# A decode step on one core: w2 loaded in four pieces in place of five, and two more unused products between the wo groups

## The chip, the core and the metric

The kernel runs on one core of one Trainium2 chip. The metric is the device time of one execution in microseconds (us). Before the change it was 84.56 us, the median of four runs (84.45, 84.47, 84.64, 84.67). A separate execution was profiled; everything that is read from the profile belongs to that one.

## The reference, cut to what matters

Four rows (a batch of 4, one token each, width 512) go through a conditioned transformer block: attention over the last 1,024 positions of a key and value cache with 32 query heads and 8 key heads, then a dense layer of width 1,792 with a ReLU. Scales, shifts and gates come from a conditioning vector `c`.

```python
mod = (_silu(c) @ w_mod).reshape(c.shape[0], 6, 1, -1)
sa, ca, ga, sb, cb, gb = (mod[:, i] for i in range(6))
h = _layernorm(x) * (1 + ca) + sa
x = x + ga * _A_ref(h, k_cache, v_cache, wq, wo)     # attention, then @ wo
h = _layernorm(x) * (1 + cb) + sb
h = jnp.einsum('bsd,df->bsf', h, w1)                 # 512 -> 1792
h = jnp.maximum(h, 0)
x = x + gb * jnp.einsum('bsf,fd->bsd', h, w2)        # 1792 -> 512
```

All weights and caches are bf16. Together the kernel reads 32 MB once.

## The kernel before

All large loads are issued by SyncE, in one queue and in the order in which they are written down: `w_mod`, two pieces of k, `wq`, six more pieces of k, eight of v, four of `wo` (one for each group g, line 121), `w1` (line 126), and `w2` in the five transfers of `W2_CHUNKS` (lines 128 to 133). A transfer is spread over the core's DMA engines. `w1` and `w2` lie in one tile, `w12`, which the profile calls `w`.

The contraction over 1,792 is cut into FT = 14 blocks of 128, numbered m = 0 to 13. A transfer of e blocks that begins at block m0 lays e consecutive rows of `w2` on each partition, so block m of that transfer holds every e-th row. The columns of `w1` that feed block m must be picked in the same way; `w1_cols` (line 477) does this with a stride of e. Thus `W2_CHUNKS` sets three things: the size of the transfers, which blocks arrive together, and the stride at which the weights of the first dense product are read.

The order of work on TensorE, VectorE, ScalarE and GpSimd is the order of the program text (a manual schedule); waits between engines are put in by the framework. What matters here is the last part, from the products with `wo` on:

1. Groups g = 0 and 1 of `wo` are multiplied with the attention result as the weights (line 427), four products side by side. The result is copied (lines 431, 432) and folded by fp32 products (line 436). Groups 2 and 3 are multiplied the other way round, with `wo` as the weights: 32 products a group of 32 columns each (line 440).
2. `keep_busy` (lines 444 to 448 and 462) issues products whose result nobody reads: an identity times columns of `wo`, into `sc_ps`, which held the attention scores earlier. It is called twice with the widths 512 and 256.
3. VectorE forms the residual and the second layer norm from `y_ps` (lines 451 to 475); TensorE sums over partitions (line 457) and puts the residual into the output's layout (`x12_ps`, line 461).
4. `ffn1` (line 489) multiplies with `w1`, once for blocks 0 to 7 and once for 8 to 13, 4 products a block (line 495); VectorE applies the norm's scale, adds, and takes the maximum with 0 (lines 498, 500, 501), which gives `uT32`.
5. The product with `w2` runs block by block through `closing` (line 192). One block is four products of 128 columns: two for x = 0 and two for x = 1, the two of a pair side by side on different quarters of the array. If `closing` is given two blocks of different halves, four products run side by side. The blocks of `ZUP` = (0, 1, 2, 3, 6, 7, 8) are summed in the upper half of the array, into `za_ps`; the others in the lower half, into `z_ps` (line 482).
6. After block 8, the last of `ZUP`, ScalarE copies `za_ps` to `zc` (line 513) and VectorE multiplies it with the gate and adds the residual (lines 514, 515). After block 13 VectorE multiplies `z_ps` with the gate (`zg`, line 520) and adds both (`res`, line 522). Two small DMAs write the result (lines 524, 525).

The order of the blocks in step 5 is written out by hand:

```python
    for ms in [(0,), (1,), (2, 4), (3, 5), (6,), (7,), (8, 9)]:
        closing([zpart(m) for m in ms])
    zc = work.tile([2 * CG, DH2], f32, name="zc")
    nc.scalar.copy(out=zc[:], in_=za_ps[2 * CG:P, :])
    ...
    for m in range(10, FT):
        closing([zpart(m)])
```

Of the kernel before, what the change touches and what calls it, by code (L numbers as in the profile page):

```python
# [17 lines left out]
def kernel(  # L18
# [14 lines left out]
    nc = tc.nc  # L33
# [8 lines left out]
    FT = Dff // P  # L42
# [63 lines left out]
    for h in range(Hkv):  # L106
        vt_ = kvpool.tile([P, NI, Dh], bf16, tag="kv", name=f"v{h}")
        nc.sync.dma_start(
            out=vt_[:].rearrange("p j d -> p (j d)"),
# [6 lines left out]
    NP = Hkv // 2  # L116
    wo_sb = wts.tile([P, NP, NL, D], bf16, tag="big", name="wo_sb")
# [7 lines left out]
    w2_sb = w12[:, DT * Dff:DT * Dff + FT * D].rearrange("p (m n) -> p m n", m=FT)  # L125
    nc.sync.dma_start(out=w1_sb, in_=B_w1.rearrange("(p t) n -> p t n", t=DT))

    W2_CHUNKS = [(0, 4), (4, 4), (8, 3), (11, 2), (13, 1)]
    assert sum(e for _, e in W2_CHUNKS) == FT
    w2_dst = w12[:, DT * Dff:DT * Dff + FT * D]  # L130
    for (m0, e) in W2_CHUNKS:
        nc.sync.dma_start(out=w2_dst[:, m0 * D:(m0 + e) * D],
# [4 lines left out]
    ident_bf = const.tile([P, P], bf16, name="ident_bf")  # L137
# [54 lines left out]
    def closing(parts):  # L192
        for x in range(NX):
            for (ps, q, j, src, rhs, start, stop, cols) in parts:
                for g in range(2):
                    q0 = (q + g) * CG
                    nc.tensor.matmul(out=ps[q0:q0 + CG, cols], lhsT=rows(src, j, x), rhs=rhs(2 * x + g),  # L197
                                     start=start and x == 0, stop=stop and x == NX - 1, tile_position=(0, q0))
# [21 lines left out]
    sc_ps = psS.tile([P, W], f32, tag="s", name="sc_ps")  # L220
# [39 lines left out]
    for t in range(DT):  # L260
        for k in range(4):
            nc.tensor.matmul(out=m4_ps[k * CG:(k + 1) * CG, :], lhsT=rows(siluT32, t, 0), rhs=wmod_sb[:, t, k * D:(k + 1) * D],
                             start=(t == 0), stop=(t == DT - 1), tile_position=(0, k * CG))
    for t in range(DT):
        nc.tensor.matmul(out=m5_ps[:], lhsT=rows(siluT32, t, 0), rhs=wmod_sb[:, t, 4 * D:5 * D],
                         start=(t == 0), stop=(t == DT - 1), tile_position=(0, 0))
# [8 lines left out]
    for t in range(DT):  # L275
        nc.tensor.matmul(out=mT[:, t, 0:4, :].rearrange("p k b -> p (k b)"), lhsT=m4_sb[:, t, :], rhs=ident_m[:],
                         start=True, stop=True)
# [45 lines left out]
    for t in range(DT):  # L323
        for hq in range(Hq):
            nc.tensor.matmul(out=qT_v[:, hq, :], lhsT=wq_sb[:, t, hq * Dh:(hq + 1) * Dh], rhs=hT[:, t, :],  # L325
                             start=(t == 0 and hq == 0), stop=(t == DT - 1 and hq == Hq - 1))
    for par in range(2):
        dst = qpad_s[:, :, par * NHW * CG:(par + 1) * NHW * CG].rearrange("p b (h c) -> p b h c", h=NHW)
        nc.vector.tensor_copy(  # L329
            out=dst[:, :, :, 16 * par:16 * par + rep],  # L330
# [78 lines left out]
    for l in range(NL):  # L409
        for a in range(2):  # L410
            for rh in range(rep // 2):
                q0 = (2 * a + rh) * CG
                nc.tensor.matmul(out=o4_ps[q0:q0 + CG, l], lhsT=sel_o[:, l].rearrange("p s d -> p (s d)"),
                                 rhs=oT_sb[:, a::2, :, :, 2 * rh:2 * rh + 2], start=True, stop=True,
# [4 lines left out]
                                   op0=ALU.mult, op1=ALU.add)  # L419


    GM = NP // 2
    y4_ps = psA.tile([P, D], f32, tag="t", name="y4_ps")
    for g in range(GM):
        for l in range(NL):
            q0 = l % 4 * CG
            nc.tensor.matmul(out=y4_ps[q0:q0 + CG, :], lhsT=o4[:, l, g % 2, g // 2, :], rhs=wo_sb[:, g, l, :],  # L427
                             start=(g == 0 and l < 4), stop=(g == GM - 1 and l >= 4), tile_position=(0, q0))
    y4 = work.tile([P, DT, P], f32, name="y4")
# [5 lines left out]
    for t in range(DT):  # L435
        nc.tensor.matmul(out=y32_ps[:, t, :], lhsT=y4[:, t, :], rhs=sel_b[:], start=(t == 0), stop=False)  # L436
    for g in range(GM, NP):
        for l in range(NL):
            for m in range(DT):
                nc.tensor.matmul(out=y32_ps[:, m, :], lhsT=wo_sb[:, g, l, m::DT], rhs=o4[:, l, g % 2, g // 2, :],  # L440
                                 start=False, stop=(g == NP - 1 and l == NL - 1 and m == DT - 1))


    def keep_busy(widths):
        for w in widths:
            nc.tensor.matmul(out=sc_ps[:, 0:w], lhsT=ident_bf[:], rhs=wo_sb[:, NP - 1, 0, 0:w], start=True, stop=True)

    keep_busy((512, 256))

    yT = work.tile([P, DT, B], f32, name="yT")  # L450
# [7 lines left out]
                     start=True, stop=True)  # L458
    x12_ps = psA.tile([2 * CG, DH2], f32, tag="t", name="x12_ps")
    for t in range(DT):  # L460
        closing([(x12_ps, 0, t, xs2, lambda j: ident_f[:, j * (P // NH):(j + 1) * (P // NH)], True, True, slice(t, None, DT))])
    keep_busy((512, 256))
    me = work.tile([P, 2, B], f32, name="me")
    nc.vector.tensor_reduce(out=me[:], in_=s2_ps[:].rearrange("p s t b -> p s b t"), axis=AX.X, op=ALU.add)
# [12 lines left out]
    def w1_cols(t, m):  # L477
        m0, e = [ch for ch in W2_CHUNKS if ch[0] <= m][-1]
        return w1_sb[:, t, m0 * P + m - m0:(m0 + e) * P:e]
# [9 lines left out]
    def ffn1(m0, m1):  # L489

        u4_ps = psA.tile([P, m1 - m0, NR, 2, B], f32, tag="t", name=f"u_ps_{m0}")
        u_ps = u4_ps[:, :, 0]
        for m in range(m0, m1):
            for t in range(DT):
                nc.tensor.matmul(out=u4_ps[:, m - m0].rearrange("p n s b -> p n (s b)"), lhsT=w1_cols(t, m),
                                 rhs=ab[:, t].rearrange("p s b -> p (s b)").unsqueeze(1).to_broadcast([P, NR, 2 * B]), start=(t == 0), stop=(t == DT - 1))
        us = work.tile([P, m1 - m0, B], f32, name=f"us_{m0}")
        nc.vector.tensor_tensor(out=us[:], in0=u_ps[:, :, 0, :], in1=rstd2[:].unsqueeze(1).to_broadcast([P, m1 - m0, B]),
                                op=ALU.mult)
        nc.vector.tensor_tensor(out=us[:], in0=us[:], in1=u_ps[:, :, 1, :], op=ALU.add)  # L500
        nc.vector.tensor_scalar_max(out=put(uT32[:, m0:m1, :]), in0=us[:], scalar1=0.0)

    def zpart(m):
        mine = ZUP if m in ZUP else ZLOW
        return (za_ps if m in ZUP else z_ps, 2 if m in ZUP else 0, m, uT32, lambda j: w2_sb[:, m, j * DH2:(j + 1) * DH2],
                m == mine[0], m == mine[-1], slice(None))

    for (m0, m1) in [(0, 8), (8, FT)]:
        ffn1(m0, m1)
    for ms in [(0,), (1,), (2, 4), (3, 5), (6,), (7,), (8, 9)]:  # L510
        closing([zpart(m) for m in ms])
    zc = work.tile([2 * CG, DH2], f32, name="zc")
    nc.scalar.copy(out=zc[:], in_=za_ps[2 * CG:P, :])
    nc.vector.tensor_tensor(out=zc[:], in0=zc[:], in1=gb2[:], op=ALU.mult)
    nc.vector.tensor_tensor(out=zc[:], in0=zc[:], in1=x12_ps[:], op=ALU.add)
    for m in range(10, FT):
        closing([zpart(m)])

    zg = work.tile([2 * CG, DH2], f32, name="zg")
# [36 lines left out]
```

## Time and profile before

| | |
|---|---|
| median of four runs | 84.56 us (84.45 to 84.67) |
| the profiled execution's own time | 84.53 us |
| its span, first to last instruction | 82.7 us |
| TensorE busy | 57.0 us, 69% |
| VectorE busy | 26.5 us, 32% |
| ScalarE busy | 23.9 us, 29% |
| mean granted TensorE clock | 0.81 of full speed |
| mean DMA rate | 388 GB/s over the span |

Some 1.8 us of the execution's own time lie outside the span. "Busy" is the time in which an engine's instructions are recorded as running; matmuls overlap, so a busy TensorE is not one at its peak. "Idle before, releaser" names what an engine waited for. PE is TensorE's products, PEld its weight loads, DVE VectorE, ACT ScalarE, SPq the queue of DMA issues on SyncE. Times in a timeline are us from the start of the span.

### The profile page before, as it was taken

How to read it: one execution, taken by the hardware profiler on the slowest of the kernel's cores; microseconds unless marked ns; L12 is line 12 of the kernel's file. 1: busy time of each engine (PE TensorE's matmuls, PEld its weight loads, DVE VectorE, ACT ScalarE, POOL GpSimd, SP SyncE). 2: the span in 40 equal slices, each digit the busy share in tenths (PEclk: the TensorE clock that was granted, in tenths of full speed). 3: DMA queues.
4: the chain of work that ended last, by engine and by line, in shares of the span. 5: the costliest groups of instructions: out<-in, count | busy, mean ns of one | idle time of the engine just before them, and what ended most of it. 6: DMA issues, size and time to landing. Idle time of an engine off the chain costs nothing.

```text
span 82.7 us, 2381 instructions
## 1 busy us (share of the span) xinstructions
PE 57.0 (69%) x1068; PEld 47.0 (57%) x1068; DVE 26.5 (32%) x76; ACT 23.9 (29%) x38; POOL 5.9 (7%) x21
## 2 busy tenths in 40 slices
PE   0001006999982798999999960999928579999740
PEld 0000006996772792997778810899918229877520
DVE  0211300348223201066654566952000320051450
ACT  3201001664302000477887745840100010002010
POOL 5895000000000000000000000000000000000000
PEclk9999999999996555599999999759855555555999
DMA  3799899998979999999999999999999999989700
GB/s 41 285 486 428 376 424 436 570 412 349 507 325 412 436 420 432 412 436 424 432 408 436 424 428 412 436 428 424 424 420 428 428 408 458 445 364 408 293 24 2
DMA packets 4257, 32.14 MB, mean 388 GB/s; under 512 B 528, under 2 KB 664, under 8 KB 1304
## 3 DMA queue, kind: packets, MB, share of 16 engines
q1 hardware_dynamic: 4192, 31.99, 92.6%
q8 instruction: 8, 0.13, 0.6%
q0 software_dynamic: 32, 0.00, 0.0%
q10 hardware_dynamic: 24, 0.01, 0.0%
q14 instruction: 1, 0.01, 0.0%
HBM read 31.99 MB, written 0.00 MB: 387 GB/s over the span
## 4 chain that ended last, share of the span: by engine, by line
DMA 93%; SPq 2%; PE 1%; DVE 1%; issue 0%
DMA v<-in_A_v_cache_dram 34%; DMA wo_sb<-in_A_wo_dram 24%; DMA w<-in_B_w_dram 19%; DMA k<-in_A_k_cache_dram 16%; PE z_ps L197 1%; SPq L86 1%; SPq L96 0%; SPq L95 0%; DVE zg L520 0%; DVE res L522 0%
## 5 line engine op out<-in xcount | busy, mean ns | idle before, releaser
L228 PE MATMUL ktp<-ident_k,k 128*128 128x128 bf16 x256 | 19.0, 246 | 5.6 <-DMA k<-in_A_k_cache_dram 5.6
L228 PEld LDWEIGHTS <-k 128*128 128x128 bf16 x256 | 17.9, 113 | 8.2 <-DMA k<-in_A_k_cache_dram 5.7
L233 ACT COPY kT<-ktp 128x1024 bf16<-128x1024 bf16 x16 | 15.6, 1015 | 18.0 <-PE ktp L228 16.9
L231 DVE COPY kT<-ktp 128x1024 bf16<-128x1024 bf16 x16 | 11.1, 691 | 17.0 <-PE ktp L228 16.7
L363 PE MATMUL oT_ps<-pT,v 128*128 128x16 bf16 x256 | 7.1, 172 | 1.6 <-issue 1.6
L363 PEld LDWEIGHTS <-v 128*128 128x128 bf16 x256 | 7.1, 100 | 1.7 <-issue 1.7
L240 PE MATMUL sc_ps<-kT,qpad 128*32 128x512 bf16 x64 | 5.6, 445 | 0.4 <-DVE qpad L329 0.4
L203 PE MATMUL tp<-ident_bf,cx_sb 8*128 8x8 bf16 x4 | 0.3, 174 | 7.2 <-DMA cx_sb<-in_A_x_dram 7.2
L380 PE MATMUL pT_ps<-ident_bf,p_rep 128*128 128x128 bf16 x32 | 3.3, 286 | 2.9 <-DVE p_rep L374 2.9
L380 PEld LDWEIGHTS <-p_rep 128*128 128x128 bf16 x32 | 2.9, 133 | 3.3 <-DVE p_rep L374 3.3
L325 PE MATMUL qT_ps<-hT,wq_sb 128*128 128x4 bf16 x128 | 3.6, 166 | 1.4 <-DVE ab L318 1.4
L325 PEld LDWEIGHTS <-wq_sb 128*128 128x128 bf16 x128 | 3.5, 104 | 1.5 <-DMA wq_sb<-in_A_wq_dram 1.5
L203 PEld LDWEIGHTS <-cx_sb 8*128 8x128 bf16 x4 | 0.2, 114 | 7.2 <-DMA cx_sb<-in_A_x_dram 7.2
L432 ACT COPY y<-y_ps 128x256 f32<-128x256 f32 x1 | 0.4, 372 | 9.0 <-DVE y L431 9.0
L374 DVE TENSOR_TENSOR p_rep<-e_sb,mi 128x512 int32<-128x512 int32 x4 | 2.5, 686 | 0.7 <-ACT e_sb L369 0.7
L405 DVE TENSOR_TENSOR oT_sb<-oT_ps,rb 128x128 bf16<-128x128 f32 x1 | 0.3, 292 | 7.5 <-PE oT_ps L363 7.5
L436 PEld LDWEIGHTS y_ps<-sel_b,y 128*128 128x128 f32 x8 | 1.8, 329 | 1.4 <-DVE y L431 1.4
L427 PE MATMUL y_ps<-wo_sb,o 128*32 128x512 bf16 x16 | 1.9, 626 | 0.9 <-DVE o L418 0.9
L440 PEld LDWEIGHTS <-wo_sb 128*128 128x128 bf16 x64 | 2.5, 121 | 0.0
L240 PEld LDWEIGHTS <-qpad 128*32 128x32 bf16 x64 | 1.3, 103 | 2.2 <-DVE qpad L329 0.7
L369 ACT ACTIVATE e_sb<-sc_ps,nb 128x256 bf16<-128x256 f32 x4 | 1.8, 471 | 2.1 <-DVE nb L346 2.1
L440 PE MATMUL y_ps<-o,wo_sb 128*128 128x32 bf16 x64 | 2.4, 195 | 0.0
(115 smaller groups left out, 56.7 us busy)
## 6 DMA issues: line engine op xcount, KB each, us to landing
k<-in_A_k_cache_dram SPq DMA_DIRECT2D x8, 1024.0 KB, 28.1
v<-in_A_v_cache_dram SPq DMA_DIRECT2D x8, 1024.0 KB, 19.6
wq_sb<-in_A_wq_dram SPq DMA_DIRECT2D x1, 4096.0 KB, 23.6
wo_sb<-in_A_wo_dram SPq DMA_DIRECT2D x4, 1024.0 KB, 19.9
wmod_sb<-in_w_mod_dram SPq DMA_DIRECT2D x1, 2304.0 KB, 9.4
w<-in_B_w_dram SPq DMA_DIRECT2D x1, 1792.0 KB
w<-in_B_w_dram SPq DMA_DIRECT2D x2, 512.0 KB, 19.8
wmod_sb<-in_w_mod_dram SPq DMA_DIRECT2D x1, 768.0 KB, 4.4
```

Of the source, the lines that this page charges most:

```text
L228: nc.tensor.transpose(out=tp[:, ii, :], in_=k_tiles[gi][:, iq * IQ + ii, :], identity=ident_k)
L231: nc.vector.tensor_copy(out=dst, in_=tp[:])
L233: nc.scalar.copy(out=dst, in_=tp[:])
L240: nc.tensor.matmul(out=sc_ps[hw * CG:(hw + 1) * CG, half * HALF:(half + 1) * HALF], lhsT=qpad[:, b, par, hw, :], rhs=kT[:, half * (NI // 2 ...
L325: nc.tensor.matmul(out=qT_v[:, hq, :], lhsT=wq_sb[:, t, hq * Dh:(hq + 1) * Dh], rhs=hT[:, t, :], start=(t == 0 and hq == 0), stop=(t == DT ...
L363: nc.tensor.matmul(out=oT_ps[:, hw, par].rearrange("p b r -> p (b r)"), lhsT=v_tiles[h][:, i, :], rhs=pT[:, i, c0:c0 + B * rep], start=(fi ...
L369: nc.scalar.activation(out=e_sb[:, ws].rearrange("q (u k e) -> q u k e", k=KC, e=2), in_=sc_ps[:, ws].rearrange("q (u e k) -> q u k e", e= ...
L374: nc.vector.tensor_tensor(out=p_w[:, ws, :], in0=e_w[:, ws].unsqueeze(2).to_broadcast([P, WQ // 2, B]), in1=mi4[:].unsqueeze(1).to_broadca ...
L380: nc.tensor.transpose(out=tp[:, ii, :], in_=p_rep[:, i // 2, :, i % 2], identity=ident_bf[:])
L427: nc.tensor.matmul(out=y4_ps[q0:q0 + CG, :], lhsT=o4[:, l, g % 2, g // 2, :], rhs=wo_sb[:, g, l, :], start=(g == 0 and l < 4), stop=(g == ...
L436: nc.tensor.matmul(out=y32_ps[:, t, :], lhsT=y4[:, t, :], rhs=sel_b[:], start=(t == 0), stop=False)
L440: nc.tensor.matmul(out=y32_ps[:, m, :], lhsT=wo_sb[:, g, l, m::DT], rhs=o4[:, l, g % 2, g // 2, :], start=False, stop=(g == NP - 1 and l = ...
```

## The change

`w2` is loaded in transfers of 6, 5, 2 and 1 blocks in place of 4, 4, 3, 2 and 1. The stride of the `w1` columns follows. Blocks 9 and 10 move: block 9 is paired with 7 and block 10 with 8, so that the copy of `za_ps` stands after blocks 0 to 10 in the text. `keep_busy` is defined earlier, takes a group number, and is called once more: two products of 256 and 128 columns, reading group 0 of `wo`, between the groups 2 and 3 of line 440.

```diff
-    W2_CHUNKS = [(0, 4), (4, 4), (8, 3), (11, 2), (13, 1)]
+    W2_CHUNKS = [(0, 6), (6, 5), (11, 2), (13, 1)]
...
+    def keep_busy(widths, g=NP - 1):
+        for w in widths:
+            nc.tensor.matmul(out=sc_ps[:, 0:w], lhsT=ident_bf[:], rhs=wo_sb[:, g, 0, 0:w], start=True, stop=True)
...
     for g in range(GM, NP):
+        if g > GM:
+            keep_busy((256, 128), 0)
         for l in range(NL):
             for m in range(DT):
                 nc.tensor.matmul(out=y32_ps[:, m, :], lhsT=wo_sb[:, g, l, m::DT], rhs=o4[:, l, g % 2, g // 2, :],
                                  start=False, stop=(g == NP - 1 and l == NL - 1 and m == DT - 1))
-
-
-    def keep_busy(widths):
-        for w in widths:
-            nc.tensor.matmul(out=sc_ps[:, 0:w], lhsT=ident_bf[:], rhs=wo_sb[:, NP - 1, 0, 0:w], start=True, stop=True)
...
-    for ms in [(0,), (1,), (2, 4), (3, 5), (6,), (7,), (8, 9)]:
+    for ms in [(0,), (1,), (2, 4), (3, 5), (6,), (7, 9), (8, 10)]:
         closing([zpart(m) for m in ms])
...
-    for m in range(10, FT):
+    for m in range(11, FT):
         closing([zpart(m)])
```

## The prediction, made before the changed kernel ran

> **What bounds the kernel now.** I read the chain of waits first, then the page's slices, then the timeline of the last 6 us, since every edit but one acts there.
>
> ```profile
> by line: DMA v<-in_A_v_cache_dram 33.9%; DMA wo_sb<-in_A_wo_dram 24.1%; DMA w<-in_B_w_dram 18.8%; DMA k<-in_A_k_cache_dram 15.9%; PE z_ps L197 0.8%; SPq L86 0.7%; SPq L96 0.5%; SPq L95 0.5%; issue 0.4%; DVE zg L520 0.4%; DVE res L522 0.3%
> ...
> 63.55 15.55 DMA w<-in_B_w_dram
> 79.10 0.04 issue
> 79.14 0.65 PE z_ps L197 x12
> ```
>
> 93% of the span is one queue of loads; only the last 1.3 us before the output belong to engines. What counts is when the last pieces of w2 land, and what follows.
>
> ```profile
> 77.76 0.39 PE L197 MATMUL za_ps<-w,uT 128*32 128x128 bf16 x8
> 78.50 0.23 PE L197 MATMUL za_ps<-w,uT 128*32 128x128 bf16 x2 [0.35 <-DMA w<-in_B_w_dram]
> ...
> 78.83 0.26 ACT L513 COPY zc<-za_ps 64x128 f32<-64x128 f32 x1 [3.64 <-PE za_ps L197]
> 79.12 0.28 DVE L514 TENSOR_TENSOR zc<-zc,gb 64x128 f32<-64x128 f32 x1 [1.46 <-ACT zc L513]
> 79.14 0.64 PE L197 MATMUL z_ps<-w,uT 128*32 128x128 bf16 x12 [0.23 <-DMA w<-in_B_w_dram]
> 79.14 0.46 PEld L197 LDWEIGHTS <-uT 128*32 128x32 bf16 x11 [0.36 <-issue]
> 79.44 0.28 DVE L515 TENSOR_TENSOR zc<-zc,x_ps 64x128 f32<-64x128 f32 x1
> 79.81 0.28 DVE L520 TENSOR_TENSOR zg<-z_ps,gb 64x128 f32<-64x128 f32 x1
> 80.13 0.28 DVE L522 TENSOR_TENSOR res<-zg,zc 64x128 bf16<-64x128 f32 x1
> ```
>
> TensorE starts blocks 8 to 10 at 78.50 and 11 to 13 at 79.14, each time because a load arrived. Two chains then meet at L520: the products of block 13, and the side chain L513, L514, L515 on what block 8 completed. L515 ends at 79.72; the gaps between dependent VectorE instructions are 0.035 us (79.405 to 79.440), so L520 could start at 79.753. It started at 79.814. **The side chain has only 0.06 us of cover.**
>
> ```profile
> 45.77:49.19 3.42, 3.18 (x52) 2.12 (x48) 1.86 (x4) 2.18 (x3) 0.00 (x0) 1.00 1.02 429
> ...
> 56.01:59.43 3.42, 3.42 (x133) 3.41 (x131) 0.40 (x2) 0.27 (x1) 0.00 (x0) 1.00 1.02 431
> 59.43:62.84 3.41, 1.80 (x69) 1.73 (x65) 0.00 (x0) 0.00 (x0) 0.00 (x0) 0.50 1.01 423
> ...
> 69.67:73.08 3.41, 3.28 (x69) 2.59 (x69) 0.61 (x4) 0.00 (x0) 0.00 (x0) 0.50 1.01 426
> 73.08:76.49 3.41, 3.41 (x78) 2.73 (x79) 0.95 (x7) 0.50 (x2) 0.00 (x0) 0.50 0.97 397
> 76.49:79.91 3.42, 2.52 (x76) 1.79 (x73) 1.69 (x9) 0.26 (x1) 0.00 (x0) 1.00 0.51 194
> ```
>
> Columns: window, length, PE busy, PEld, DVE, ACT, POOL, granted clock, DMA share, GB/s. The clock changes only on this 3.41 us grid. The w2 products ran at full clock because it rose at 76.49, after a window in which PE was busy throughout; the window before it, 0.13 us short of full, didn't raise it.
>
> **What the Trainium skill says.** "TensorE: Matmul & The Clock Gate", Part 1, says that the clock is halved until a window of about 3.4 us has been busy, and that these windows run free of the kernel's start. The spacing agrees; that the phase differs between runs, one profile can't show. The same page, "Architectural detail", says that VectorE takes its instructions strictly in order: L520 indeed stands behind L514 and L515. "DMA: Bandwidth & Descriptors", "Why a DMA increments its semaphore by 16 and not by 1", says that the engines of one transfer finish independently. Agreed: the sixteen completions of the last transfer are spread from 77.59 to 79.45 us, so the latest engine decides. The same page, "Anatomy of one DMA", gives a fixed cost of about 2 us a transfer; this trace doesn't show that in a full queue, where the last transfers complete 0.35 us apart.
>
> **One transfer fewer.** In the packet records the latest engine completes w1 at 75.08 and the w2 transfers at 76.30, 77.53, 78.46, 79.10 and 79.45: 1.22, 1.24, 0.93, 0.64 and 0.345 us for 4, 4, 3, 2 and 1 blocks. That is 0.294 us a block plus 0.05 us a transfer. The packets say the same: 46, 84, 121, 159 ns for 1, 2, 3, 4 KB, and 234 for the 6 KB packets of w_mod; straight lines with 8 ns over, times 8 packets an engine. Hence 6 blocks cost 1.81 and 5 cost 1.52: completions at 76.89, 78.41, 79.05 and 79.40. **Gain 0.047 us on the last two landings**; bounds 0 and 0.10. The issues cost nothing: the last w2 issue ends at 66.31, 11 us before its first data moved.
>
> **Blocks 6 to 10 wait together.** Before, at the third transfer's landing only blocks 8, 9, 10 were open, and block 8 went first: first product 78.502, last one for za 78.571. Now 6, then 7 with 9, then 8 with 10. At full clock a step of `closing` is 53 to 56 ns (77.250, 77.306, 77.362, 77.418), two steps a call, so block 8's last product is the sixth step: five steps, 0.275 us, after the first. First product: 78.413 plus 0.042 (landing to product, the same at 79.100/79.141 and 79.445/79.487) is 78.455. Last za product 78.730, 0.220 long, 0.037 to the copy: L513 at 78.987 (before 78.828). From the starts before, L513 to L514 is 0.294, L514 to L515 0.318, and the next another 0.318: **L520 can't start before 79.917**. The z side: 79.398 plus 0.042 plus 0.070 to the last product, plus 0.219, plus 0.038: 79.767. That wait is over earlier than before, and the side chain is late in its place. Blocks 11 and 12 still start at their landing, since block 10 is issued by 78.75.
>
> L520 moves from 79.814 to 79.917: **+0.10 us**. From there to the end (L522, the output DMAs) nothing changes.
>
> **The unused products.** TensorE waited for group 3 of wo between its products at 70.771 and 70.880. The 512-column product held PE 0.38 to 0.40 us until the next start, so 256 and 128 take about 0.20 and 0.10 at half clock, 0.30 in all; starting at 70.80, they end at 71.10 and push group 3 back by 0.22 us. Queued behind: the two later fillers, the norm's sum (L457), the residual's turn, w1's products. The chain moves along to the second filler, which then frees PE at about 75.27 instead of 75.05. w1's products began at 75.125, released by w1's landing at 75.08; they start 0.15 late, at 75.28, and uT at 77.27 instead of 77.13. Blocks 0 to 5 take four calls, 0.45 us, until about 77.8, and the next landing is 78.41. **0.6 us of cover: cost nothing.** Without it, 0.15 us. Weight loads at strides of 6 and 5 elements are not in the trace; those at 4 (118 ns, half clock) and at 3, 2, 1 (95 to 110, full clock) don't depend on the stride, so I take 0, bounds 0 and 0.3.
>
> What they do to the clock is the open part. Counting columns streamed per window (fp32 as four passes), 69.67 to 73.08 had 71% and didn't raise the clock, 73.08 to 76.49 had 80% and did; a full clock was taken away after 37% and kept after 44%. With the fillers the first window has some 77%: the clock may rise at 73.08 already. The next one, faster and with a wait of about 0.7 us for w1, falls to some 47%: just enough to keep it.
>
> **Sum.** 84.53 + 0.10 = 84.63 for the profiled execution. That lies 0.03 under the median of the runs shown, so for the median I predict 84.56 + 0.10 = **84.66 us**, 0.12% up. A measurement of this kernel can tell about 0.2%, 0.17 us, from no change: 84.39 to 84.73 counts as the same.
>
> **Rivals.**
> - *The clock is low when blocks 6 to 10 run* (slower). If the fillers raise the clock a window early and it is taken back, or the phase is unlucky, a step costs 107 ns. Then block 8's last product is 0.535 after the first and about 0.27 long: L520 at about 80.23, +0.41; against a kernel before that is also at half clock (about 79.98) +0.25. Time 84.8 to 84.97. It decides once the clock falls before 78.4. For it: the 47% against 44%, and that six steps now stand where two stood. Against: the same fillers make a rise by 76.49 likelier.
> - *The clock becomes steadier* (faster). The runs before fall into 84.45 and 84.65; the same sum for a half-clocked end before gives 0.17 to 0.18 us. If that pair is a late clock and the fillers cure it, the median falls by some 0.1 of its own while the side chain adds 0.1; with a transfer gain of 0.10 in place of 0.05 the result is 84.35 to 84.5. For it: the two pairs. Against: the side chain takes back most.
> - *The strides slow the weight loads*: 44 loads of blocks 0 to 10, twice their 33 ns, are 1.45 us, less 0.6 of cover: 85.3. Nothing in the trace speaks for it.
>
> **Chances.** Forecast 0.53, low clock 0.25, steadier clock 0.20, strides 0.02. The forecast's own range is 84.55 to 84.78: of its 0.53, 0.38 lies within 0.2%, 0.13 above, 0.02 below. Low clock: 0.23 above, 0.02 within. Steadier clock: 0.10 below, 0.10 within. Strides: above. Together faster 0.12, same 0.50, slower 0.38. The range 84.42 to 84.97 leaves a tenth on each side.
>
> **What would show it.** Right: in the timeline after, L520 begins 0.03 to 0.04 after L515's end, the products of blocks 11 to 13 lie well before it, and the wait for w2 before block 6 ends near 78.4; the last product with w2 starts some 0.05 earlier than before. The first filler starts at 70.8 and w1's products at about 75.3. The clock is 1.00 in the window that holds 78.5. Wrong: L520 still follows the last z product (then the 0.275 is too long), or steps of 107 ns after 78.4, or landings that move by more than 0.1.

## The result: slower by 0.38%, and the profile after

The changed kernel took 84.92 us (median of 34 runs, 84.43 to 85.27) against 84.57 us before (53 runs, 84.24 to 84.93): a ratio of 1.0038, 95% interval 1.0029 to 1.0047. (Ratios here and below are given as the record has them, beside the medians; they aren't the quotients of these medians.) Its profiled execution took 84.84 us with a span of 83.0 (before 84.53 and 82.7).

The end of the chain of waits of the changed kernel (start, length, what):

```profile
53.36 21.55 DMA w<-in_B_w_dram
74.96 2.44 PE u_ps L497 x56
77.40 0.37 PE za_ps L197 x3
...
78.96 0.21 PE za_ps L197 x4
79.19 0.27 ACT zc L515
79.48 0.29 DVE zc L516
79.80 0.28 DVE zc L517
80.08 0.21 DVE zg L522
80.31 0.28 DVE res L524
```

Before, this chain stayed on the loads until 79.10. Now the view has it leave them at 74.96, when w1 has landed, and run through engines alone: w1's products, the w2 products summed in za, and the side chain over `zc` to `res`. One wait it doesn't show, since the recorded lengths of products overlap. By their starts, block 3's last product began at 78.11 and block 6's first at 78.32, where steps are 0.107 us apart; the load of blocks 6 to 10 landed at 78.28. So block 6 still waited for its load, and what came before it isn't what makes the end late. The last w2 load, landed at 79.21, isn't on it: `zg` (line 520 before, 522 in the changed kernel) began 0.79 us after that landing, where before it was 0.37.

Three stretches of the 3.41 us grid in the changed kernel (window, length, then PE, PEld, DVE, ACT, POOL, granted clock, DMA share, GB/s):

```profile
68.97:72.38 3.41, 3.41 (x71) 2.94 (x71) 0.28 (x2) 0.00 (x0) 0.00 (x0) 0.50 1.02 435
72.38:75.80 3.42, 2.49 (x56) 1.85 (x55) 1.27 (x9) 0.50 (x2) 0.00 (x0) 1.00 0.97 402
75.80:79.21 3.41, 3.41 (x92) 3.17 (x92) 1.13 (x6) 0.02 (x1) 0.00 (x0) 0.50 0.66 258
```

The clock rose at 72.38, was taken back at 75.80, and the w2 products ran at half speed until 79.21, where before they had 1.00. The edges of the grid lie elsewhere than before (75.80 for 76.49): its phase does differ from one execution to the next.

And w1's products alone. The number to read is the count of products in a window; first the changed kernel, in which 75.00 to 75.80 holds blocks 0 to 5, 76.10 to 76.90 blocks 6 to 10, and 76.90 to 77.30 the last three:

```profile
75.00:75.80 0.80, 0.80 (x18) 0.80 (x19) 1.00 1.01 425
76.10:76.90 0.80, 0.80 (x25) 0.80 (x24) 0.50 0.99 399
76.90:77.30 0.40, 0.40 (x16) 0.37 (x14) 0.50 0.99 384
```

Then the kernel before, blocks 0 to 7 and, at the same half clock, 8 to 10:

```profile
75.20:76.00 0.80, 0.80 (x26) 0.80 (x27) 0.50 1.04 424
76.22:76.45 0.23, 0.23 (x14) 0.23 (x12) 0.50 0.94 379
```

The counts take in a few products that overlap an edge; start to start in the two traces, a product takes 46 to 48 ns at a stride of 6, 40 at 5, 33 at 4, 28 at 3 and 27 at 2. The 47 ns at stride 6 stand here at full clock; the kernel before with the new strides (part 2) has the same at half clock. From the first start to the last, w1's 56 products took 2.24 us in place of 1.70, and the first part of uT was ready 2.42 us after w1's landing in place of 2.05.

So several things are different at once: fewer transfers, the order of the blocks, the new unused products (below also "fillers"), the strides with a later uT, and the clock. The experiments take them apart. Each has its own runs of the kernel before beside it (medians 84.43 to 84.48); a profile of each kernel shows one execution, and so one phase of the clock's grid only.

### The profile page after: what moved, and what is told of

Read it like the earlier page. It is cut to its first block, busy times and chain, and to the rows that moved or that the text cites. A ratio compares the mean times of both kernels' runs of the same rounds, so it can differ in the third digit from the quotient of the medians.

```text
span 83.0 us, 2384 instructions
## 1 busy us (share of the span) xinstructions
PE 56.7 (68%) x1070; PEld 47.3 (57%) x1070; DVE 26.5 (32%) x76; ACT 23.9 (29%) x38; POOL 5.9 (7%) x21
## 4 chain that ended last, share of the span: by engine, by line
DMA 63%; PE 26%; DVE 4%; issue 1%; SPq 1%; ACT 1%; DVEq 0%
DMA w<-in_B_w_dram 26%; DMA v<-in_A_v_cache_dram 24%; DMA k<-in_A_k_cache_dram 14%; PE ktp L228 8%; PE qT_ps L325 4%; PE u_ps L497 3%; PE sc_ps L240 2%; PE za_ps L197 2%; PE mT L276 2%; PE mT L278 2%; PE m_ps L262 1%; PE m_ps L265 1%; PE st_ps_var L292 1%; PE gb_ps L197 1%; SPq L96 0%
## 5 line engine op out<-in xcount | busy, mean ns | idle before, releaser
L497 PEld LDWEIGHTS <-w 128*128 128x128 bf16 x56 | 2.3, 131 | 1.1 <-DMA w<-in_B_w_dram 1.1
L497 PE MATMUL u_ps<-ab,w 128*128 128x32 bf16 x56 | 2.4, 197 | 0.7 <-DMA w<-in_B_w_dram 0.7
```

## Experiments

**1. The fillers alone, all but the fillers, and a longer filler.** My first theory was the low-clock rival, with the new fillers to blame, since the clock in the profile after did what that rival says.

```diff
 # fillers alone: the kernel before, with
+        if g > GM:
+            keep_busy((256, 128), 0)
 # all but the fillers: the changed kernel, with
-        if g > GM:
-            keep_busy((256, 128), 0)
 # longer filler: the changed kernel, with, before w1's products
-    keep_busy((512, 256))
+    keep_busy((512, 512, 512))
```

Expected of the fillers alone:

> The kernel before with only the two unused products (256 and 128 columns) between groups 2 and 3 of wo; transfers and block order as before. Clock theory (the fillers raise the clock one window early, the wait for w1 then takes it back, and the w2 blocks run at half clock): slower, but by less than the whole change, +0.1 to +0.2 us, since only two steps of block 8 and the later blocks are stretched; where the window of 78.5 us is granted 0.50, the steps there are 107 ns. Order theory (the regrouping of blocks 6 to 10 costs the time at any clock): no change, within 0.05 us of before. Load theory (six- and five-block transfers land late): no change.

Measured: 84.51 us against 84.43, ratio 1.0008 (0.9998 to 1.0018). That can't be told from no change, and lies under what the clock theory asked. In its profile the clock was 1.00 from 77.58 on, after the first two w2 blocks, and the timeline's end is that of the kernel before:

```profile
78.48 0.23 PE L197 MATMUL za_ps<-w,uT 128*32 128x128 bf16 x2 [0.32 <-DMA w<-in_B_w_dram]
...
79.42 0.28 DVE L517 TENSOR_TENSOR zc<-zc,x_ps 64x128 f32<-64x128 f32 x1
79.80 0.28 DVE L522 TENSOR_TENSOR zg<-z_ps,gb 64x128 f32<-64x128 f32 x1
```

Expected of the change without the fillers (transfers, order and strides stay):

> The changed kernel without the two new unused products; transfers of 6, 5, 2 and 1 and the new block order stay. Clock theory: the clock is as before in most runs, so within 0.1 us of before (-0.05 to +0.10), with a tail of slower runs where the free-running window falls badly. Order theory: nearly the whole loss stays, +0.25 to +0.35 us, with L520's successor (zg) waiting for the side chain at a clock of 1.00. Load theory: the loss stays too, and the last landing is later than before relative to w1's landing.

Measured: 84.93 against 84.43, ratio 1.0050 (1.0031 to 1.0069). The whole loss is here, without a filler. Nor do the loads come late: the last landed 4.30 us after w1, against 4.37 before. But the clock isn't 1.00, as the order theory wanted. The two windows of its grid that hold w1's and w2's products:

```profile
73.02:76.43 3.41, 3.41 (x69) 2.63 (x69) 0.95 (x6) 0.50 (x2) 0.00 (x0) 0.50 0.97 407
76.43:79.85 3.42, 3.33 (x84) 2.83 (x82) 1.47 (x8) 0.26 (x1) 0.00 (x0) 0.50 0.49 186
```

The first one was busy throughout, as in the kernel before between 73.08 and 76.49, and yet the clock didn't rise at its end. What differs is what PE was busy with: w1's products waited for their weights. Counted as in the prediction, some 70% of that window streamed columns, against some 80% before.

Expected of the longer filler:

> The changed kernel with the second filler call, the one before w1's products, made of three products of 512 columns in place of 512 and 256, to fill the wait for w1 (0.72 us idle in the changed kernel's profile) and so keep the clock. Clock theory: the window that holds 78.5 us is granted 1.00, steps of 53 to 56 ns, zg is released by the z products or within 0.05 us of them; time within 0.1 us of before, 0.25 to 0.4 us under the changed kernel. Where the clock is low during the fillers they take 1.28 us and delay w1's products by some 0.8 us, which is just hidden. Order theory and load theory: as slow as the changed kernel, +0.35 us.

Measured: 84.69 against 84.43, ratio 1.0041 (1.0024 to 1.0059), with three runs of 85.2 to 85.4. It missed: in its profile, which is one of these three, the clock was half during the three fillers, so that w1's products began 0.62 us after w1's landing (0.05 in the changed kernel), and the clock stayed at half to the end. It can't tell the theories apart.

After these runs the theory had to be another: the strides slow the weight loads, and this both delays uT and thins out the streamed share, which the clock seems to follow.

**2. The strides alone, all but the strides, and two other layouts.** In the first two, the columns of w1 no longer match the rows of w2, so the second dense product is computed on other rows; the work is the same.

```diff
 # strides alone: the kernel before, with
-        m0, e = [ch for ch in W2_CHUNKS if ch[0] <= m][-1]
+        m0, e = [ch for ch in [(0, 6), (6, 5), (11, 2), (13, 1)] if ch[0] <= m][-1]
 # all but the strides: the changed kernel, with
-        m0, e = [ch for ch in W2_CHUNKS if ch[0] <= m][-1]
+        m0, e = [ch for ch in [(0, 4), (4, 4), (8, 3), (11, 2), (13, 1)] if ch[0] <= m][-1]
```

Expected of the strides alone:

> The kernel before, with transfers, block order and fillers as before; only the columns of w1 are read at the strides of the changed kernel, 6 for blocks 0 to 5, 5 for 6 to 10, so that the blocks of w1 no longer match the rows of w2 (the second dense product is computed on other rows). Stride theory (formed after the second run: a weight load at stride e holds PE 47 ns for 6 and 40 for 5 against 33 for 4; w1's products take 0.5 us longer, uT comes 0.35 us later, and the window's streamed share falls so that the clock isn't raised before the w2 products): +0.15 to +0.35 us, clock 0.50 at 78.5 us, w1's products 2.4 us long in place of 1.87. Order theory (the regrouping of blocks 6 to 10 costs the time at any clock): within 0.05 us of before.

Measured: 84.66 against 84.48, ratio 1.0020 (1.0008 to 1.0032); 11 of its 20 runs lie within 0.2 us of the median before, 9 above. In its profile w1's products took 2.24 us, the clock stayed at half until 79.16, and zg began 0.60 us after the last landing. The loss is in the expected range, at its lower end.

Expected of all but the strides:

> The changed kernel with its transfers, block order and fillers; only the columns of w1 are read at the strides of the kernel before (4, 4, 3, 2, 1), so that the blocks of w1 no longer match the rows of w2 (the second dense product is computed on other rows). Stride theory: nearly all of the loss is gone: -0.05 to +0.10 us against before, the last landing about 0.05 us sooner after w1's, w1's products 1.5 to 1.9 us long, uT as early as before. Order theory: +0.35 us stays, with the side chain deciding. If both are needed (late uT or low clock, and the six steps), this one and the one with the new strides alone both lie well under +0.35.

Measured: 84.52 against 84.48, ratio 1.0009 (0.9998 to 1.0020). The new transfers, the new order and the fillers together cost nothing that can be told apart as long as the strides are the old ones. Its profile caught a run with the clock low all the same (84.68 us), and there zg began 0.74 us after the last landing (79.18), with uT early (2.06 us after w1's landing):

```profile
75.48:78.90 3.42, 2.99 (x91) 2.65 (x88) 1.06 (x6) 0.00 (x0) 0.00 (x0) 0.50 0.76 298
...
78.27 0.29 PE L197 MATMUL za_ps<-w,uT 128*32 128x128 bf16 x2 [0.26 <-DMA w<-in_B_w_dram]
...
79.92 0.28 DVE L522 TENSOR_TENSOR zg<-z_ps,gb 64x128 f32<-64x128 f32 x1
```

The low clock with the six steps gives nearly the whole 0.79 of the changed kernel. In 16 of the 22 runs of this kernel the time was within 0.2 us of the median before; in the changed kernel in 7 of 34.

The next two keep the reference whole. The first lays the six blocks out as two runs of three rows (stride 3), the second joins the first two transfers of the kernel before to one of eight blocks, two runs of four:

```diff
+        k = W2_RUN.get(m0, e)
-        nc.sync.dma_start(out=w2_dst[:, m0 * D:(m0 + e) * D],
-                          in_=B_w2[m0 * P:(m0 + e) * P, :].rearrange("(q e) n -> q (e n)", e=e))
+        nc.sync.dma_start(out=w2_dst[:, m0 * D:(m0 + e) * D].rearrange("q (h x) -> q h x", x=k * D),
+                          in_=B_w2[m0 * P:(m0 + e) * P, :].rearrange("(h q e) n -> q h (e n)", e=k, q=P))
```

Expected of the two runs of three:

> The changed kernel with the six-block transfer laid out as two runs of three rows on each partition (still one transfer, 3 KB packets in place of 6 KB), so that blocks 0 to 5 are read at stride 3; blocks 6 to 10 stay at stride 5. The whole reference is computed. Stride theory: most of the loss goes: blocks 0 to 5 at 28 ns a load in place of 47, w1's products about 1.9 us, time +0.0 to +0.15 us. The six-block transfer lands up to 0.06 us later (8 more packets an engine at 8 ns). Order theory: +0.35 us stays.

Measured: 84.75 against 84.48, ratio 1.0029 (1.0010 to 1.0048), in 8 runs from 84.43 to 85.06. The median is worse than expected, while the interval reaches into what was expected. In its profile the clock was 1.00 from 77.54 on, w1's products took 1.76 us, and zg began 0.46 us after the last landing; that is 0.10 us later after w1's landing than before (4.84 against 4.74). This execution took 84.91 us, 0.38 more than the profiled one before. Of the rest, 0.13 stands in w1, which landed at 75.21 (74.84 to 75.09 in the other profiles of this case), and most of what is left lies outside the span. Why, no run shows, and how often this kernel met a low clock isn't known either.

Expected of the eight blocks:

> The kernel before with its first two transfers of four blocks joined into one of eight (two runs of four rows a partition, 4 KB packets, stride 4 as before); block order and fillers as before; the whole reference is computed. One transfer fewer is worth about 0.05 us on the last landings: -0.05 us, with blocks 0 to 7 all waiting for the landing near 77.5 us. At a low clock their six steps of 0.21 us run past the next landing and the gain turns into a loss of 0.1 to 0.3 us in those runs. Order theory has no say here; a loss at full clock would speak for late landings.

Measured: 84.92 against 84.48, ratio 1.0047 (1.0030 to 1.0064). A miss in the median: what I had expected for some runs held for all six. No block can start before the landing at 77.54, TensorE then goes from block to block at half clock until block 8's last product at 79.02, and zg begins 0.79 us after the last landing. Old strides, and the same loss: here too blocks that wait together ran at a low clock. That all six runs met one isn't shown; the profile is of one.

**3. Late uT or low clock?** The strides do both. To part them: no fillers at all, which keeps the clock low, and more columns per weight load, which raises the streamed share and leaves uT late.

```diff
 # no fillers: the kernel before, and the changed one without its new call too
-    keep_busy((512, 256))
 # more columns: NR copies of the activations per weight load
-    NR = 4
+    NR = 5    # in the kernel before
+    NR = 6    # in the changed kernel
```

Expected of the kernel before without fillers, and of the changed one:

> The kernel before without any of its filler products (both calls of keep_busy taken out), so that the clock is low in the w2 products in nearly every run. Clock theory, as it stands now (the new strides slow w1's weight loads, which both streams less per window and delays uT; the clock is then low when blocks 6 to 10 run, and their six steps put the side chain on the path): +0.15 to +0.25 us over before, since at 107 ns a step blocks 11, 12 and 13 finish some 0.2 us late. Late-uT theory (the delay of uT by itself carries the loss, the clock doesn't matter): within 0.05 us of before.

> The changed kernel without any filler products (all three calls of keep_busy taken out): low clock in nearly every run. Clock theory: about as slow as the changed kernel, +0.30 to +0.40 us over before, and 0.10 to 0.20 us over the kernel before without fillers; that difference is what the six steps cost at a low clock. Late-uT theory: +0.35 us over before and over the kernel before without fillers alike.

Measured: 84.62 against 84.43 for the first, ratio 1.0014 (1.0000 to 1.0027), and 84.95 for the second, 1.0060 (1.0047 to 1.0072). Both profiles had half clock in the w2 products. zg began 0.57 us after the last landing in the first and 0.78 in the second. So a low clock costs 0.1 to 0.2 us in the kernel before, and some 0.3 us more in the changed one, with its order, strides and transfers. That is more than the 0.10 to 0.20 I had expected, and by the medians it is as much as the late-uT theory said. What speaks against that theory is the loss in the first of the two, where uT wasn't late, and that block 6 began at its landing in the second.

The profiles part the low clock, the order and the strides better. One execution for each row; the last two columns are the start of the side chain's last step (L515 before) and of zg, in us after the last landing:

| kernel | order | strides | clock in blocks 6 to 10 | side chain's last step | zg |
|---|---|---|---|---|---|
| before | old | old | 1.00 | 0.00 | 0.37 |
| before, no fillers | old | old | 0.50 | 0.13 | 0.57 |
| strides alone | old | new | 0.50 | 0.40 | 0.60 |
| all but the strides | new | old | 0.50 | 0.54 | 0.74 |
| changed | new | new | 0.50 | 0.59 | 0.79 |
| changed, no fillers | new | new | 0.50 | 0.57 | 0.78 |
| changed, six copies (below) | new | new | 1.00 | 0.25 | 0.46 |

In the first two rows block 13 decides when zg begins, and the low clock, in the second to the end, costs 0.20 us there. In the other five the side chain decides: zg begins 0.20 us after its last step. In the four with the new order block 6 began 0.04 us after its landing, with uT early or late. A late uT is hidden there, and what counts is the six steps, of 107 ns at half clock. With the old order and new strides the blocks ran without a pause from 77.57 to 78.94, and there it is the late uT, at a low clock, that holds block 8 up. At full clock new order and new strides together cost 0.09.

Expected of more columns in the kernel before:

> The kernel before with five in place of four copies of the activations streamed against each w1 weight load (NR 5, products of 40 columns in place of 32; the extra copy isn't read, the reference is computed). At half clock 40 columns take as long as a weight load at stride 4, so blocks 0 to 7 cost the same and stream more. Clock theory: the clock is raised before the w2 products in more runs: -0.05 to -0.10 us, the slower runs of before become rarer. Late-uT theory: 0 to +0.05 us, since blocks 8 to 13 take 0.1 us longer.

Measured: 84.49 against 84.43, ratio 1.0005 (0.9996 to 1.0014): no gain, which misses the clock theory's figure and is what the late-uT theory said. 51 of the 53 runs of the kernel before in the first comparison lie no more than 0.2 us above their median; there was little to cure.

Expected of more columns in the changed kernel:

> The changed kernel with six copies of the activations per w1 weight load (NR 6, products of 48 columns; the extra copies aren't read, the reference is computed). At half clock 48 columns take 40 ns, which hides behind the 47 and 40 ns of the weight loads at strides 6 and 5; only blocks 11 to 13 get longer, by 0.16 us. The strides, the order and the transfers of the change stay. Clock theory: the streamed share rises to 85 to 100% in w1's products, the clock is raised before blocks 6 to 10 in most runs, and the loss falls to +0.05 to +0.20 us. Late-uT theory: uT comes as late as in the changed kernel or later, and the loss stays at +0.35 us or grows.

Measured: 84.59 against 84.43, ratio 1.0030 (1.0020 to 1.0041); 12 of 22 runs lie within 0.2 us of the median before. By the medians the loss is in the expected range, by the ratio at its upper end or above it. The intervals of this ratio and the changed kernel's overlap; the changed kernel without fillers, measured beside it on the same chip, lies clear above. The timeline of its profiled execution, which took 84.36 us, the fastest of its runs:

```profile
74.88 2.40 PE L497 MATMUL u_ps<-ab,w 128*128 128x48 bf16 x56 [0.29 <-DMA w<-in_B_w_dram]
...
77.05 0.20 DVE L503 TENSOR_SCALAR uT<-us 128x32 bf16<-128x32 f32 x1
...
78.23 0.23 PE L197 MATMUL za_ps<-w,uT 128*32 128x128 bf16 x2 [0.30 <-DMA w<-in_B_w_dram]
...
78.79 0.26 ACT L515 COPY zc<-za_ps 64x128 f32<-64x128 f32 x1 [3.57 <-PE za_ps L197]
...
79.08 0.28 DVE L516 TENSOR_TENSOR zc<-zc,gb 64x128 f32<-64x128 f32 x1 [1.14 <-ACT zc L515]
79.40 0.28 DVE L517 TENSOR_TENSOR zc<-zc,x_ps 64x128 f32<-64x128 f32 x1
79.60 0.28 DVE L522 TENSOR_TENSOR zg<-z_ps,gb 64x128 f32<-64x128 f32 x1
```

w1's products are as long as in the changed kernel, and uT is ready as late after w1's landing (2.42 us in both). Block 6 waits for its load, longer than there, and zg begins 4.77 us after w1's landing, against 5.09 in the changed kernel and 4.74 before. The clock is what is different:

```profile
73.04:76.45 3.41, 3.01 (x71) 2.57 (x72) 1.00 (x7) 0.50 (x2) 0.00 (x0) 1.00 0.97 405
76.45:79.87 3.42, 2.58 (x82) 1.93 (x79) 1.89 (x9) 0.26 (x1) 0.00 (x0) 1.00 0.49 189
```

A late uT alone therefore costs nearly nothing; it is the low clock, with six steps before the side chain, that carries the loss of the changed kernel. Whether the six copies kept the clock here, or a phase that put more of w1's products into the first of these windows, one profile can't show. No version tried beat the kernel before.

## Why the prediction was half right

The 84.92 us lie inside the whole range given, 84.42 to 84.97, but above the forecast's own 84.55 to 84.78, and where the low-clock rival put them. Of the signs named, a clock of 1.00 at 78.5 us failed to come (it was 0.50), and steps of 107 ns after 78.4, a sign of being wrong, did.

- **One transfer fewer.** Predicted 0.047 us sooner. From w1's landing to the last landing the six profiles with transfers of 6, 5, 2 and 1 blocks at one run a partition have 4.30 to 4.38 us, mean 4.325; the five with the old transfers 4.32 to 4.42, mean 4.379: 0.054. Right in the mean; the two ranges overlap.
- **Nothing changes from L522 to the end.** Wrong, and put at nothing without a reason. From the start of `res` to the end of the span the five profiles with five w2 transfers have 2.59 to 2.61 us, the eight with four 2.65 to 2.68. The output's landing isn't later (1.70 to 1.71 us after the start of `res` in all thirteen), but of SyncE's last waits one more stands behind it in the kernels with four. That is some 0.06 us, as much as the missing transfer saves. Why it goes with the number of loads, no run shows.
- **The side chain at full clock.** Predicted: L520 0.52 us after the last landing, +0.10 in all. In the run with NR 6 it was 0.456, and from w1's landing it was late by 0.03 (4.77 against 4.74). The direction was right. The mis-sized term is the last 0.318: I took L520 to follow L515 as L515 follows L514. It doesn't read what L515 writes, and it started 0.20 us after L515's start, while L515 still ran (79.40 and 79.60 above). That also means the cover before the change was 0.17 us, not 0.06. From w1's landing to the end of the span this run is 0.08 us longer than before, close to the +0.10, but by luck: the 0.07 too much on VectorE and the 0.06 missing at the end nearly cancel.
- **The unused products cost nothing.** Right, by the run with the fillers alone. The late start that was worked out for w1's products, 0.15 us, didn't come: they began 0.05 us after w1's landing in its profile, as before.
- **The strides.** "I take 0, bounds 0 and 0.3" is the step that failed. I compared the recorded length of a weight load, 118 against 95 to 110 ns, and blamed the clock for the difference, though the loads at stride 3 ran at half clock nearly to the last, as those at 4 did. What counts is the spacing, and the trace before had a warning: 33 ns at stride 4 and 28 at 3, at the same half clock. The runs showed 40 and 47 for 5 and 6, about 6.7 ns for each unit of stride from 4 on, and 0.5 us over blocks 0 to 10. The cover for a late uT held, as block 6 still began at its landing. What the 0 left out is what the slower products do to the clock. The rival on strides named the right instruction, put 1.45 us on it and gave it 0.02 (and 84.56 + 1.45 - 0.6 is 85.4, not 85.3).
- **The clock.** The slower rival said a low clock before 78.4 us, 107 ns a step, L520 at 80.23 and 84.8 to 84.97 us. The changed kernel had zg at 80.00 (w1 landed 0.17 us sooner) and 84.92. The low clock and the size were right, and its chance, 0.25, too small, because the cause I gave for it was wrong: the fillers, or an unlucky phase. In the profile after, the clock did rise a window early, and it was lost again at 75.80. But without the new fillers the loss stayed, and with the old strides it went. Its chain was right as well: block 6 began 0.04 us after its landing, and block 8's last product 0.49 after that, where the rival had 0.535.
- **The clock becomes steadier.** It didn't. The two pairs of times before were chance: 53 runs fill the range from 84.24 to 84.93 without a gap at 84.55.

The forecast of 84.66 thus had the sum of a run at full clock, while most runs of the changed kernel seem to have been of the other kind: 27 of 34 lie over 0.2 us above the median before. That these are the runs with a low clock in the w2 products is inferred from the profiles. For the timed runs only the mean clock of the whole span is on record, and it doesn't sort them: runs at 0.835 and 0.836 took 84.60 and 85.27 us.

## What to carry to other kernels

When a transfer's size also sets the stride at which weights are read, price the stride by the start-to-start spacing of the products, at one clock, not by the length of the loads. Work that waits for one late landing together was cheap here only at full clock; where the clock follows the share of time in which TensorE streams columns, as the windows here suggest, a slower weight load one stage earlier can take it away. A sum made at one clock state needs its counterpart at the other before a chance is put on it.

## What the runs showed of the hardware that was not expected

- Products of 32 columns, each with its own 128x128 bf16 weights, start every 24 to 30 ns, mostly 26 to 28, up to a stride of 3 elements, and every 33, 40 and 47 ns at 4, 5 and 6; the 47 was the same at full and at half clock.
- "Busy" doesn't tell what the clock will do: before the change it was lost at 59.43 after a window in which PE was busy throughout. By the streamed share (columns over the granted rate, fp32 as four passes), windows at half clock with up to some 76% were followed by half clock and those with 77% or more by full, with two exceptions, windows of 73% that held w2 products side by side and were followed by full; a full clock was lost after 38% or less, and kept after 43% or more. This is read from the records of thirteen profiles, by a count that is good to two or three points only, and nothing was set up to find the limits.
- An instruction on VectorE that doesn't depend on the one before starts 0.20 us after that one's start, a dependent one 0.32 (64x128 fp32, 0.28 us long; the 0.20 between L517 and L522 above).
- The last transfer's landing isn't the end of what a transfer costs: with one load fewer in the queue, 0.05 us was gained at the landing and 0.06 lost in the waits that close the program.
